# Two key chunks per visit in an attention that runs beside a mixer, and key bucket numbers by three products

## Chip, core and metric

The kernel runs on one NeuronCore of a Trainium2 chip. The metric is the device time of the program in microseconds. A core has TensorE (matrix products, PE in the profile), VectorE (DVE), ScalarE (ACT), GpSimd (POOL) and SyncE (SP, which issues most DMAs). Products are written to PSUM, which has eight banks; everything else lies in SBUF.

## What is computed

A hashed attention, followed by a Fourier mixer with a two-layer perceptron. The attention has 4 batches, 8 heads, 768 rows of 64 channels. Each query and key row gets a bucket number from 6 sign bits, and a query weighs only the keys of its own bucket:

```python
q_bits = (np.einsum('bhsd,dk->bhsk', q, proj) > 0).astype(np.int64)
k_bits = (np.einsum('bhsd,dk->bhsk', k, proj) > 0).astype(np.int64)
q_bucket = np.sum(q_bits * powers, axis=-1)
k_bucket = np.sum(k_bits * powers, axis=-1)
mask = q_bucket[:, :, :, None] == k_bucket[:, :, None, :]
scores = np.where(mask, scale * np.matmul(q, k.transpose(0, 1, 3, 2)), -1000000000.0)
attn = softmax(scores)            # written out in the reference
out = np.matmul(attn, v)
```

The result, as 4 x 768 rows of 512 channels, goes through

```python
mixed = np.real(np.fft.fft(np.fft.fft(x, axis=1), axis=2))
u = x + mixed
un = (u - mu) / np.sqrt(var + 1e-06)
return u + np.maximum(un @ w_ch1, 0.0) @ w_ch2
```

## The kernel before

Heads go in pairs: pair n = 0 to 15, four pairs a batch, `n // 4` the batch. The two heads of a pair lie on partitions 0 to 63 and 64 to 127. Keys are cut into six chunks c of 128, queries into two halves g of 384.

One visit of the attention, for one pair and one chunk, does this. `weigh` (L871) issues four score products (L893), 64 rows deep, so that the two heads run side by side in the array, each query half into one PSUM tile of two banks from the pool `ps_sc` (two such tiles). ScalarE takes the exponential of each half (L897) into a weights buffer `pk`; there are two of these, used in turn. For pairs 5 to 15 VectorE then masks the weights, one instruction per head (L903): it compares the bucket numbers of the queries, `qb`, with that of the key on each partition, `kb`, and multiplies. VectorE adds the masked weights to `acc` (L988), from which the row sums come. `values` (L909) later issues four products of the weights with v (L914), 64 columns wide, so that here too the two heads run side by side, into two PSUM banks from `ps_o` that gather all six chunks. After the last chunk `scale` (L919) adds up `acc` by products with ones (L932) and divides.

Every f32 product shows in the profile as two passes, so a visit's scores are 8 instructions, and its values too.

In `attention` (L955) the values of a chunk are issued in the visit after its own: a visit is scores of c, then values of c-1. The list `pending` holds what is still to do. After each visit the generator yields, and the main loop (L1500 on) issues a few steps of the mixer of the batch before, about 2.3 a visit: these are called fill below. Fill goes through stages: folds, `cs` products (L1086, emptied by ScalarE), A and B products (L1115, both emptied by VectorE, L1129), first-layer products (L1390, emptied by ScalarE, with sums on VectorE), second-layer products (L1270, emptied half by VectorE, L1282, half by ScalarE). All their PSUM tiles come from `pt`, during the attention from a pool `ps_1` of two banks. The generator `ahead` = `prepare(n+1)` (L755) is advanced in chunks 1 to 5; it makes the next pair's transposed q and k, the sign bits (L825, one bank of `ps_1`), `qb` (L839, two tiles of `ps_sc`) and `kb` (L849, one tile of `ps_sc`, copied to SBUF by VectorE at L853).

The order on each engine in batches 1 to 3 is made by a planner, ahead of time: at each moment it issues the instruction, among those that it reckons ready, that stands first in the program. Two things change that. `issue_after` puts an instruction behind a given one on its engine, and `high_priority` moves it ahead of what stands up to 500 places before it. `behind()` does both with the matmul kept in `last[0]`; in batches 1 to 3 it glues the scores of a visit together (all but the first) and the values to them. In batch 0 the order is the program's own. Batches 0 and 1 have other surroundings: loads and conversions of the weights run beside them.

Of the kernel before, what the change touches and what calls it, by code (L numbers as in the profile page):

```python
# [11 lines left out]
F32 = mybir.dt.float32  # L12
# [8 lines left out]
P = 128  # L21
# [464 lines left out]
def _main(  # L486
# [112 lines left out]
    for h in range(2):  # L599
        nc.sync.dma_start(pj[h * D : (h + 1) * D, h * NBITS : (h + 1) * NBITS], proj)  # L600
    pw = const.tile([P, 2, P], BF16, tag="pw", name="pw")
    ones = const.tile([P, 32], F32, tag="ones", name="ones")
    nc.gpsimd.memset(ones, 1.0)
    mhalf = const.tile([P, 1], F32, tag="mhalf", name="mhalf")
# [150 lines left out]
    def prepare(n):  # L755

        lite = n in LITE
        ts = {}
        for io, nm in enumerate("qk"):
            tn = nat.pop((nm, n))  # L760
            tt = wt([P, S], F32, nm + "t", f"{nm}t{n}")
            if n > 0:
                to, at = tt, tn
                if nm == "q":

                    to = tt.rearrange("p (i r n) -> p r i n", i=2, r=2)
                    at = tn.rearrange("p (r i n) -> p r i n", i=2, r=2)
                nc.vector.transpose(to, at)
            for g in range(2) if n == 0 else ():
                ps = pt([P, 3, P], f"tr{nm}{n}_{g}")  # L770
                for i in range(3):
                    c = 2 * i + g if nm == "q" else 3 * g + i
                    nc.tensor.transpose(ps[:, i, :], tn[:, c * P : (c + 1) * P], ident)
                if nm == "q":
                    for i in range(2):
                        dst = tt[:, i * HALF + g * HALF // 2 : i * HALF + (g + 1) * HALF // 2]
                        evac(
                            dst.rearrange("p (j c) -> p c j", c=3),
                            ps[:, :, i * D : (i + 1) * D],
                        )  # L780
                else:
                    evac(
                        tt[:, g * HALF : (g + 1) * HALF],
                        ps.rearrange("p c t -> p (c t)"),
                    )
            ts[nm] = tt
            yield
            norm(n, io, tn)
        if lite:

            qk = wt([P, 2, S], BF16, "qb", f"qkb{n}")
            qz = qk[:, 0].rearrange("p (g s) -> p g s", g=2)
            bits = {"q": qz[:, 0], "k": qk[:, 1, 0:HALF]}
            for io, nm in enumerate("qk"):
                ps = pt([P, HALF], f"bits{nm}{n}")
                for j in range(4):
                    h, g = divmod(j, 2)  # L800
                    nc.tensor.matmul(
                        ps[32 * j : 32 * j + 32, :], pjw[:, h * D : h * D + 32],
                        ts[nm][:, g * HALF : (g + 1) * HALF], start=True, stop=True,
                    )
                nc.vector.tensor_scalar(
                    bits[nm], ps, 0.0, off[:, io : io + 1],
                    op0=ALU.is_gt, op1=ALU.subtract,
                )
                if io == 0:
                    for g in (1, 0):  # L810
                        nc.vector.tensor_scalar(
                            qz[:, g], qz[:, 0], own[:, g : g + 1], None, op0=ALU.mult
                        )
                else:
                    for j in range(4):
                        to, at = (slice(32 * i, 32 * i + 32) for i in (j, j ^ 1))
                        nc.vector.tensor_copy(qk[to, 1, HALF:S], qk[at, 1, 0:HALF])
                yield
            preps[n] = ts["q"], ts["k"], qk, None
            return  # L820

        ps = pt([P, HALF], f"bits{n}")
        for j in range(4):
            src = ts["qk"[j // 2]][:, (j % 2) * HALF : (j % 2 + 1) * HALF]
            nc.tensor.matmul(  # L825
                ps[32 * j : 32 * j + 32, :], pj, src, start=True, stop=True
            )
        bt = wt([P, HALF], BF16, "bt", f"bt{n}")
        nc.vector.tensor_scalar(bt, ps, 0.0, None, op0=ALU.is_gt)  # L829
        yield  # L830

        qb = wt([P, 2, S], BF16, "qb", f"qb{n}")
        kb = wt([P, 2, NT], F32, "kb", f"kb{n}")
        for h in range(2):
            ps = ps_sc.tile([P, 2, 512], F32, tag="sc", name=f"qb{n}_{h}")
            for g in range(2):
                rows = slice(32 * g, 32 * g + 32)
                with behind() if g + h else nullcontext():
                    last[0] = nc.tensor.matmul(  # L839
                        ps[:, g, 0:HALF], pw[rows, h, :], bt[rows, :],  # L840
                        start=True, stop=True,
                    )
            evac(qb[:, h, :].rearrange("p (g s) -> p g s", g=2), ps[:, :, 0:HALF])
        ps = ps_sc.tile([P, 2, 512], F32, tag="sc", name=f"kb{n}")
        for c in range(NT):
            g, i = divmod(c, NT // 2)
            rows = slice(64 + 32 * g, 96 + 32 * g)
            with behind() if c else nullcontext():
                last[0] = nc.tensor.matmul(  # L849
                    ps[:, g, 2 * i : 2 * i + 2], bt[rows, i * P : (i + 1) * P],  # L850
                    pw[rows, :, 0], start=True, stop=True,
                )
        nc.vector.tensor_copy(  # L853
            kb.rearrange("p h (g i) -> p g i h", g=2),
            ps[:, :, 0:NT].rearrange("p g (i h) -> p g i h", h=2),
        )
        preps[n] = ts["q"], ts["k"], qb, kb

# [6 lines left out]
    @contextmanager  # L865
    def behind():

        with tc.issue_after(last[0].ins), tc.high_priority(offset=AHEAD):
            yield

    def weigh(n, c):  # L871

        qt, kt, qb, kb = preps[n]
        ks = slice(c * P, (c + 1) * P)
        heads = [slice(h * D, (h + 1) * D) for h in range(2)]
        pk = pks[npk[0] % NPK]
        npk[0] += 1
        for g in range(2):
            qs = slice(g * HALF, (g + 1) * HALF)
            ps = ps_sc.tile([P, 2, 512], F32, tag="sc", name=f"sc{n}_{g}_{c}")  # L880
            if kb is None:

                at = (c + (NT // 2 if g else 0)) % NT * P
                for h, rows in enumerate(heads):
                    nc.tensor.matmul(
                        ps[:, h, 0:HALF], qb[rows, 1, at : at + P],
                        qb[rows, 0, g * HALF : (g + 1) * HALF],
                        start=True, stop=False,
                    )

            for h, rows in enumerate(heads):
                with behind() if g + h and n >= NPAIR else nullcontext():
                    last[0] = nc.tensor.matmul(  # L893
                        ps[:, h, 0:HALF], kt[rows, ks], qt[rows, qs],
                        start=kb is not None, stop=True,
                    )
            nc.scalar.activation(  # L897
                pk[:, g, :, 0:HALF], ps[:, :, 0:HALF], AF.Exp, scale=SCALE
            )
        if kb is not None:  # L900
            for h in range(2):
                w = pk[:, :, h, 0:HALF]
# [6 lines left out]
    def values(n, c, pk, oos):  # L909

        for g in range(2):
            w = HALF + 1 - g
            for h in range(2):
                nc.tensor.matmul(  # L914
                    oos[g][h * D : (h + 1) * D, 0:w], nat["v", n][:, (2 * c + h) * D : (2 * c + h + 1) * D],
                    pk[:, g, h, 0:w], start=(c == 0), stop=(c == NT - 1),
                )

    def scale(n, oos, sums):  # L919

# [34 lines left out]
    def attention(b):  # L955
# [11 lines left out]
        for t in range(NPAIR):  # L967
# [5 lines left out]
            oos = [ps_o.tile([P, 512], F32, tag="o", name=f"oo{n}_{g}") for g in range(2)]  # L973
            acc = wt([P, 2, 2, HALF], F32, "acc", f"acc{n}", 1)
            first = None
            for c in range(NT):
                pk = weigh(n, c)
                new = pk[:, :, :, 0:HALF]
                sums = [acc]
                if c == 0:  # L980
# [4 lines left out]
                else:  # L985

                    for g in (0, 1) if b == 0 else (slice(0, 2),):
                        nc.vector.tensor_tensor(  # L988
                            acc[:, g], (first if c == 1 else acc)[:, g], new[:, g],
                            op=ALU.add,  # L990
                        )

                for sc in scales:
                    next(sc, None)
                scales.clear()
                while pending:
                    finish()
                for sc in scales if b else ():
                    next(sc, None)
                pending.append((n, c, pk, oos, sums))  # L1000
                if c > (3 if b == 1 else 2):
                    next(half, None)
                if c > 0:
# [477 lines left out]
    with tc.manual_schedule(engines={ET.PE, ET.DVE, ET.Activation, ET.Pool}):  # L1481
# [8 lines left out]
        pwf = wt([P, 2, P], F32, "ef", "pwf", 1)  # L1490
        nc.sync.dma_start(pwf, cn["pw"].ap())
        nc.scalar.copy(pw, pwf)
        means = []
        late = [(f, average(f)) for f in range(DFF // 2, DFF, WC)]
        for _, avg in late:
# [98 lines left out]
```

## Time and profile before

| | us |
|---|---|
| median of 3 runs | 1098.81 |
| lowest and highest | 1097.87, 1100.31 |
| the profiled execution | 1099.06 |
| its span in the trace | 1097.1 |
| TensorE busy | 1044.5 |
| VectorE busy | 790.7 |
| ScalarE busy | 499.3 |
| score products L893, busy | 155.3 |
| value products L914, busy (two forms) | 91.0 + 85.4 |
| exponentials L897, one | 0.81 |
| mask L903, one of a visit's two | 1.01 |
| sum L988, over both halves | 1.75 |

The span is what the profiler saw from the first to the last instruction; the time has about 2 us around it. In a line of the timeline the columns are start, length, engine, line, operation, what is written and read, rows x columns of the array, shape, and how many instructions were merged; brackets hold the idle time before and what ended it. The ends of matmuls are modelled, so what an operation costs TensorE is read from start to start.

### The profile page before, as it was taken

The page shows a single profiled execution, that of the slowest core. Times are in us where ns is not written, and L with a number is a line of the kernel's source. Part 1 is how long each engine was busy: PE and PEld are TensorE (multiplying, and loading weights), DVE is VectorE, ACT ScalarE, POOL GpSimd, SP SyncE. Part 2 cuts the span into 40 slices and gives each one's busy share as a digit, 9 for nine tenths or more (in the row PEclk, how much of TensorE's full clock was granted, in tenths as well). Part 3 has the DMA queues.
Part 4 walks back from the last instruction along what each step waited for, and adds up shares of the span by engine and source line. Part 5 has one row for each costly group of instructions (what it writes and reads, how often), then busy time and mean ns, then how long its engine had stood idle before and what let it go on. Part 6 is the DMA issues. An engine that isn't in the chain of part 4 may idle for free.

```text
span 1097.1 us, 14139 instructions
## 1 busy us (share of the span) xinstructions
PE 1044.5 (95%) x4933; PEld 633.2 (58%) x4933; DVE 790.7 (72%) x1336; ACT 499.3 (46%) x1055; POOL 58.4 (5%) x132
## 2 busy tenths in 40 slices
PE   7989897999989999999999999999999999999997
PEld 3333354446744675545664576645674569768676
DVE  5899958878599977776767785965856775744353
ACT  6987555653276324454326433355315532341430
POOL 0000000002000020010000011001000002100000
PEclk9999999999999999999999999999999999999999
DMA  9755353450056161322144134213032205122401
GB/s 225 222 96 126 63 133 79 141 168 13 20 155 209 45 203 24 68 63 66 26 157 108 48 74 161 44 39 95 16 119 75 68 28 173 50 86 71 140 20 41
DMA packets 175710, 103.13 MB, mean 94 GB/s; under 512 B 129552, under 2 KB 162960, under 8 KB 175632
## 3 DMA queue, kind: packets, MB, share of 16 engines
q1 hardware_dynamic: 169840, 88.65, 30.2%
q0 software_dynamic: 4224, 13.11, 3.7%
q8 instruction: 41, 0.67, 0.3%
q10 hardware_dynamic: 1568, 0.39, 0.2%
q14 instruction: 37, 0.30, 0.1%
HBM read 81.14 MB, written 20.97 MB: 93 GB/s over the span
## 4 chain that ended last, share of the span: by engine, by line
PE 61%; DVE 12%; ACT 4%; issue 2%; DMA 2%; DVEq 0%; SPq 0%; ACTq 0%
PE o L1270 23%; PE h_p L1390 19%; PE oo L914 6%; PE sc L893 6%; DVE pk L903 3%; PE cs L1086 2%; PE A L1115 2%; DMA zraw<-in_moe_w_ch_dram 2%; PE B L1115 1%; DVE acc L988 1%; ACT rr L948 1%; DVE w L1282 1%; DVE h L1256 1%; PE bits L825 1%; PE un L1141 1%
## 5 line engine op out<-in xcount | busy, mean ns | idle before, releaser
L1270 PE MATMUL o<-w,h 128*128 128x256 f32 x1152 | 259.4, 382 | 1.2 <-ACT tq L1289 0.7
L1270 PEld LDWEIGHTS o<-w,h 128*128 128x128 f32 x1152 | 216.3, 190 | 43.6 <-issue 4.6
L897 ACT ACTIVATE pk<-sc 128x768 f32<-128x768 f32 x192 | 147.4, 808 | 77.8 <-PE sc L893 60.2
L1390 PE MATMUL h_p<-x,w 128*128 128x384 f32 x448 | 163.3, 494 | 2.9 <-ACT h L1412 1.5
L914 PE MATMUL oo<-pk,vn 128*64 128x385 f32 (+1 forms) x768 | 155.8, 500 | 5.9 <-DVE pk L903 3.3
L893 PE MATMUL sc<-qt,kt 64*128 64x384 f32 x768 | 155.3, 507 | 5.6 <-ACT pk L897 5.3
L903 DVE SCALAR_TENSOR_TENSOR pk<-qb,kb,pk 128x768 f32<-128x768 bf16 x132 | 129.0, 1013 | 29.9 <-ACT pk L897 29.7
L1390 PEld LDWEIGHTS h_p<-x,w 128*128 128x128 f32 x448 | 82.3, 190 | 70.4 <-ACT pk L897 5.4
L988 DVE TENSOR_TENSOR acc<-acc,pk 128x1536 f32<-128x1536 f32 (+1 forms) x72 | 105.7, 1482 | 7.2 <-ACT pk L897 6.7
L1390 PE MATMUL h_p<-w 128*128 128x384 f32 x288 | 105.5, 489 | 2.3 <-ACT w L1427 2.3
L914 PEld LDWEIGHTS oo<-pk,vn 128*64 128x64 f32 x768 | 49.1, 136 | 100.0 <-issue 69.8
L893 PEld LDWEIGHTS sc<-qt,kt 64*128 64x128 f32 x768 | 66.9, 188 | 50.3 <-issue 23.1
L1390 PEld LDWEIGHTS h_p<-w 128*128 128x128 f32 x288 | 53.7, 190 | 41.7 <-ACT w L1427 3.5
L1282 DVE SCALAR_TENSOR_TENSOR w<-o,rs,w 128x256 f32<-128x256 f32 x56 | 26.7, 479 | 41.6 <-PE o L1270 41.6
L1300 ACT COPY tq<-o 128x256 f32<-128x256 f32 x24 | 8.9, 372 | 105.0 <-PE o L1270 105.0
L1270 PE MATMUL o<-w 128*128 128x256 f32 x176 | 42.3, 383 | 1.3 <-DVE w L1282 1.3
L1416 DVE TENSOR_TENSOR h<-h 128x384 f32<-128x384 f32 x32 | 17.8, 556 | 32.7 <-ACT h L1415 32.7
L1289 ACT COPY tq<-o 128x256 f32<-128x256 f32 x24 | 8.9, 371 | 69.3 <-PE o L1270 69.3
L1270 PEld LDWEIGHTS o<-w 128*128 128x128 f32 x176 | 32.8, 190 | 8.8 <-DVE w L1282 2.9
L1423 DVE TENSOR_TENSOR h<-h 128x384 f32<-128x384 f32 x32 | 17.7, 553 | 27.0 <-ACT h L1422 27.0
L1024 POOL DMA_DIRECT2D out_dram<-w x30 | 16.3, 547 | 388.7 <-issue 293.2
L1086 PE MATMUL cs<-ch,z 128*128 128x128 f32 (+3 forms) x192 | 33.6, 327 | 3.0 <-DVE bt L829 1.9
(170 smaller groups left out, 1314.1 us busy)
## 6 DMA issues: line engine op xcount, KB each, us to landing
w<-ad SPq DMA_DIRECT2D x168, 128.0 KB, 2.0
w<-bd SPq DMA_DIRECT2D x42, 512.0 KB, 4.6
zraw<-in_moe_w_ch_dram POOLq DMA_DIRECT2D x16, 512.0 KB, 3.9
bd<-w SPq DMA_DIRECT2D x14, 512.0 KB, 4.0
vn<-in_v_dram SPq DMA_DIRECT2D x32, 192.0 KB, 3.3
qn<-in_q_dram SPq DMA_DIRECT2D x120, 48.0 KB, 2.4
kn<-in_k_dram SPq DMA_DIRECT2D x60, 96.0 KB, 3.3
zraw<-in_moe_w_ch_dram SPq DMA_DIRECT2D x8, 512.0 KB, 5.9
```

The lines of the kernel that those rows point to most:

```text
L893: last[0] = nc.tensor.matmul(ps[:, h, 0:HALF], kt[rows, ks], qt[rows, qs], start=kb is not None, stop=True,)
L897: nc.scalar.activation(pk[:, g, :, 0:HALF], ps[:, :, 0:HALF], AF.Exp, scale=SCALE)
L903: nc.vector.scalar_tensor_tensor(w, qb[:, h].rearrange("p (g s) -> p g s", g=2), kb[:, h, c : c + 1], w, op0=ALU.is_equal, op1=ALU.mult,)
L914: nc.tensor.matmul(oos[g][h * D : (h + 1) * D, 0:w], nat["v", n][:, (2 * c + h) * D : (2 * c + h + 1) * D], pk[:, g, h, 0:w], start=(c == ...
L988: nc.vector.tensor_tensor(acc[:, g], (first if c == 1 else acc)[:, g], new[:, g], op=ALU.add,)
L1086: nc.tensor.matmul(ps[:, pc + 2 * lo : pc + 2 * hi - 1 : 2], z[:, cp, pc, par, t * P : (t + 1) * P], ch[:, cp, pc, lo:hi], start=(cp == 0) ...
L1115: nc.tensor.matmul(ps[:, cols], F[:, par, k, t, j * P : (j + 1) * P], sq[:, t, k, cols], start=(t == 0), stop=(t == 1),)
L1270: nc.tensor.matmul(ps, a[:, r], right7[i][:, r], start=start and r == 0, stop=r == HF // 2 - 1, skip_group_check=not start,)
L1282: nc.vector.scalar_tensor_tensor(t[:, cols], src, r, t[:, cols], op0=ALU.mult, op1=ALU.add)
L1390: nc.tensor.matmul(ps, left[:, k], right[i][:, k], start=start and k == 0, stop=k == 1, skip_group_check=not start,)
L1416: nc.vector.tensor_tensor(c21, c12, c21, op=ALU.add)
L1423: nc.vector.tensor_tensor(c22, c21, c22, op=ALU.add)
```

## The change

In batches 2 and 3 (pairs from `TWO = 8`) a visit takes two chunks: scores of c, values of c-2 and of c-1, scores of c+1, in this order and glued; then two rounds of fill, since the loop still yields once a chunk. The exponentials of c come between the two values in the program, so that the values of c-2 have read the weights buffer that they write. Batches 0 and 1 keep one chunk a visit.

The key bucket numbers: instead of six products of 32 rows, in a score tile, three products of all 128 rows with a weight matrix `pwk` of two columns for each half, zero outside the rows of that half, in a tile of `ps_1`. The query bits' rows meet zeros.

```diff
+    pwk = const.tile([P, 2, 2], BF16, tag="pwk", name="pwk")
+    nc.gpsimd.memset(pwk, 0.0)
...
-        ps = ps_sc.tile([P, 2, 512], F32, tag="sc", name=f"kb{n}")
-        for c in range(NT):
-            g, i = divmod(c, NT // 2)
-            rows = slice(64 + 32 * g, 96 + 32 * g)
-            with behind() if c else nullcontext():
-                last[0] = nc.tensor.matmul(
-                    ps[:, g, 2 * i : 2 * i + 2], bt[rows, i * P : (i + 1) * P],
-                    pw[rows, :, 0], start=True, stop=True,
-                )
+        ps = pt([P, NT // 2, 2, 2], f"kb{n}")
+        for i in range(NT // 2):
+            nc.tensor.matmul(
+                ps[:, i], bt[:, i * P : (i + 1) * P], pwk, start=True, stop=True
+            )
...
-    def weigh(n, c):
+    TWO = 8
+
+    def scores(n, c, glued=False):
...
-                with behind() if g + h and n >= NPAIR else nullcontext():
+                with behind() if (g + h or glued) and n >= NPAIR else nullcontext():
...
-            nc.scalar.activation(
-                pk[:, g, :, 0:HALF], ps[:, :, 0:HALF], AF.Exp, scale=SCALE
-            )
+            if n < TWO:
+                weights(pks[npk[0] % NPK], g, ps)
+            pss.append(ps)
+        return pss
+
+    def weights(pk, g, ps):
+
+        nc.scalar.activation(
+            pk[:, g, :, 0:HALF], ps[:, :, 0:HALF], AF.Exp, scale=SCALE
+        )
+
+    def weigh(n, c, pss):
+
+        qb, kb = preps[n][2:]
+        pk = pks[npk[0] % NPK]
+        npk[0] += 1
+        for g in range(2) if n >= TWO else ():
+            weights(pk, g, pss[g])
...
-                nc.tensor.matmul(
+                oo = nc.tensor.matmul(
...
+        last[0] = oo
...
-            for c in range(NT):
-                pk = weigh(n, c)
+            def chunk(c, pss):
+
+                nonlocal first
+                pk = weigh(n, c, pss)
...
+                elif c % 2 == 0:
+                    pss = scores(n, c)
+                    if len(pending) > 1:
+                        finish()
+                    new = [chunk(c, pss)]
+                    if pending:
+                        finish()
+                    new.append(chunk(c + 1, scores(n, c + 1, True)))
+                    for sc in scales:
+                        next(sc, None)
+                    scales.clear()
+                    pending += new
...
+        for g in range(2):
+            rows = slice(64 + 32 * g, 96 + 32 * g)
+            nc.scalar.copy(pwk[rows, g], pwf[rows, :, 0])
```

`chunk` is the old body of the loop up to the sum into `acc`; `finish` takes the oldest entry of `pending` and issues its values, and after a pair's last chunk its `scale`.

More of the change, by code (lines that the diff above doesn't have):

```diff
@@ L843, in prepare @@
             evac(qb[:, h, :].rearrange("p (g s) -> p g s", g=2), ps[:, :, 0:HALF])
-        ps = ps_sc.tile([P, 2, 512], F32, tag="sc", name=f"kb{n}")
-        for c in range(NT):
-            g, i = divmod(c, NT // 2)
-            rows = slice(64 + 32 * g, 96 + 32 * g)
-            with behind() if c else nullcontext():
-                last[0] = nc.tensor.matmul(
-                    ps[:, g, 2 * i : 2 * i + 2], bt[rows, i * P : (i + 1) * P],
-                    pw[rows, :, 0], start=True, stop=True,
-                )
+        ps = pt([P, NT // 2, 2, 2], f"kb{n}")
[3 more added lines that the diff above has]
+            )
         nc.vector.tensor_copy(
             kb.rearrange("p h (g i) -> p g i h", g=2),
-            ps[:, :, 0:NT].rearrange("p g (i h) -> p g i h", h=2),
+            ps.rearrange("p i g h -> p g i h"),
         )
@@ L869, in behind @@
             yield
-    def weigh(n, c):
+    TWO = 8
+    def scores(n, c, glued=False):
         qt, kt, qb, kb = preps[n]
+        pss = []
         ks = slice(c * P, (c + 1) * P)
         heads = [slice(h * D, (h + 1) * D) for h in range(2)]
-        pk = pks[npk[0] % NPK]
-        npk[0] += 1
         for g in range(2):
@@ L991, in attention @@
                         )
[L993 to L1000, printed above, removed]
+                return n, c, pk, oos, sums
+            for c in range(NT):
+                if n < TWO:
+                    new = chunk(c, scores(n, c))
+                    for sc in scales:
+                        next(sc, None)
+                    scales.clear()
+                    while pending:
+                        finish()
+                    for sc in scales if b else ():
+                        next(sc, None)
+                    pending.append(new)
+                elif c % 2 == 0:
[4 more added lines that the diff above has]
+                    if pending:
+                        finish()
+                    new.append(chunk(c + 1, scores(n, c + 1, True)))
+                    for sc in scales:
+                        next(sc, None)
+                    scales.clear()
+                    pending += new
                 if c > (3 if b == 1 else 2):
```

## The prediction

> **What bounds the kernel now.** I read the page first (busy shares and the 40 slices), then the chain of waits, then the timeline of TensorE around several visits of the attention, then a table of stretches for VectorE. The page:
>
> ```profile
> PE 1044.5 (95%) x4933; PEld 633.2 (58%) x4933; DVE 790.7 (72%) x1336; ACT 499.3 (46%) x1055; POOL 58.4 (5%) x132
> ...
> PE   7989897999989999999999999999999999999997
> ...
> PE 61%; DVE 12%; ACT 4%; issue 2%; DMA 2%; DVEq 0%; SPq 0%; ACTq 0%
> ```
>
> The attention of batches 2 and 3 runs from 407 to about 923 us beside the mix of the batch before; there every slice of TensorE is a 9, and the end is set by TensorE. But its matmul ends are modelled, so "busy" hides the price of a change of array shape. That price is read from the starts of groups:
>
> ```profile
> 521.64 3.72 PE L1270 MATMUL o<-w,h 128*128 128x256 f32 x16
> 525.29 1.56 PE L893 MATMUL sc<-qt,kt 64*128 64x384 f32 x8
> 526.78 1.51 PE L914 MATMUL oo<-pk,vn 128*64 128x385 f32 x8
> 528.22 3.72 PE L1270 MATMUL o<-w,h 128*128 128x256 f32 x16
> ```
>
> A pass over 384 columns takes 0.32 us in a long run (the chain of waits has L1390 x112 in 36.12 us), one over 256 columns 0.213. The 8 score passes run in pairs side by side (64 rows each), so they stream 4 x 0.32 = 1.28 us; the next group starts 1.49 after them: 0.21 is lost. The 8 value passes also stream 1.28, and the next starts 1.44 later: 0.16 lost. The 16 passes of fill stream 3.41 and scores follow at 3.65: 0.24 lost. So each visit pays fill to scores 0.24, scores to values 0.21, values to fill 0.16: 0.61 us. I worked out the same differences from all starts between 415 and 945 us; they repeat within some hundredths almost everywhere, and waits over 0.4 us there add up to under 10 us. The two transitions that the change brings in are in the trace too:
>
> ```profile
> 407.31 1.56 PE L893 MATMUL sc<-qt,kt 64*128 64x384 f32 x8
> 408.80 1.16 PE L1086 MATMUL cs<-ch,z 128*128 128x129 f32 x8
> ...
> 97.11 1.51 PE L914 MATMUL oo<-pk,vn 128*64 128x385 f32 x8
> 98.55 0.34 PE L885 MATMUL sc<-qkb 64*128 64x384 bf16 x2
> ```
>
> Scores to fill costs 1.49 - 1.28 = 0.21, values to scores 1.44 - 1.28 = 0.16 (to the bf16 scores of batch 0, same shape of array as the f32 ones).
>
> **What the Trainium skill says.** "TensorEngine Tiling (Array Packing)", Key Properties: changing the tiling mode drains the TensorE, changing the tile within it does not. The trace agrees: 0.16 to 0.24 us at each change of shape, none between passes of one shape. The same page, Gotcha 1: row tiles write to different PSUM banks, which raises the pressure on PSUM; here the two score tiles take four of the eight banks. "TensorE: Matmul & The Clock Gate", Architectural detail: ScalarE and VectorE are strict FIFOs, so whatever is queued behind a mask waits for it.
>
> **The change part by part.** Sums are made against the profiled execution, 1099.06 us (span 1097.1 and 1.96 around it); the median of the runs is 1098.81, so the two agree within 0.3.
>
> (1) Fewer changes of shape. Per two chunks before: 2 x 0.61 = 1.22. After: fill to scores 0.24, scores to values 0.21, values to values 0, values to scores 0.16, scores to fill 0.21 = 0.82. A batch before: 0.45 for its first chunk (no values yet), 23 x 0.61, and 0.40 for the values left at its end: 14.9. After: 0.45, 11 x 0.82, 0.40: 9.9. Saved 5.0 a batch, 10.0 for two. The passes themselves, exponentials, masks and sums stay the same in number; no DMA is moved past another, though each load of the next pair stands beside visits at other times.
>
> Does the second group of scores find its buffers free? Both score buffers are filled by the first chunk. Put its start at 0: scores end at about 0.9 and 1.5; the exponential of query half 0 also needs the weights buffer that the values of chunk c-2 read, free at 1.49 + 0.69 + about 0.17 = 2.35. It takes 0.81 (the page's 808 ns), so the two end near 3.2 and 4.0. The 16 value passes end at 1.49 + 2.56 = 4.05; the new scores start at 4.21 and 4.85. Slack about 0.85: one ScalarE copy of 0.48 in between fits, two do not. Then fill is put between, and a break costs 0.16 + 0.24 - 0.16 = 0.24. Before, 4 of 46 visits are broken (scores x4, A/B products x2, scores x4 at 437.28 is one). I take 4 breaks of 24: give back 1.0.
>
> (2) A stage where VectorE sets the pace gains nothing:
>
> ```profile
> 430.00:440.00 10.00, 9.11 (x58) 6.64 (x58) 9.48 (x15) 1.94 (x3) 0.00 (x0) 1.00 0.00 0
> 440.00:450.00 10.00, 10.00 (x60) 6.75 (x58) 10.00 (x14) 3.12 (x6) 0.00 (x0) 1.00 0.40 75
> ```
>
> (columns: us, then busy us of PE, PEld, DVE.) In the A/B stage VectorE is at 9.5 to 10 of 10; there are four chunks, so two double visits, a batch: 4 x 0.41 = give back 1.6.
>
> (3) Key bucket numbers. Before, six products of 32 rows between fill; starts 566.42 and 566.58 with fill at 564.93 ahead give fill to them 0.21 and them to fill 0.16 in all: 0.37 per pair. After, three bf16 products over the full array, no change of shape; the trace has no such product of 2 columns. Bounds: a bf16 weight load of half the rows takes 0.09 (L885), so three exposed ones 0.28, none exposed about 0.05. I take 0.27; saved 0.10 x 11 pairs = 1.1 (bounds 1.0 and 3.5). They leave the score buffers too, and with that this wait goes, seen in both batches:
>
> ```profile
> 432.92 0.50 PE L839 MATMUL qb<-bt,pw 32*128 32x384 bf16 x4
> 434.31 0.24 PE L849 MATMUL kb<-pw,bt 32*128 32x2 bf16 x6 [0.89 <-ACT qb L537]
> ```
>
> 2 x 0.89 = 1.8. What is late next there is the copy of the key numbers on VectorE, behind masks, holding one of the two banks that fill uses; that is in (4). The set-up (one GpSimd fill, two ScalarE copies of 32 x 2, nearest row 0.197) lies at about 119 us beside weight loads, where nobody waited for the copy of pw: 0, at most 0.4.
>
> (4) The new wait. Masks 2 x 1.01 and a sum of 1.75 make 3.8 us of VectorE per chunk; two chunks in a row make 7.6. Fill has two PSUM banks, and the second-product steps (L1270) empty half of their banks on VectorE. Before:
>
> ```profile
> 510.77 1.90 DVE L903 SCALAR_TENSOR_TENSOR pk<-qb,kb,pk 128x768 f32<-128x768 bf16 x2
> 512.59 0.68 DVE L1256 TENSOR_TENSOR h<-h 128x512 f32<-128x512 f32 x1
> 513.20 1.75 DVE L988 TENSOR_TENSOR acc<-acc,pk 128x1536 f32<-128x1536 f32 x1
> ...
> 516.00 1.99 PE L1270 MATMUL o<-w 128*128 128x256 f32 x8 [0.55 <-DVE w L1282]
> ```
>
> Already a burst of 3.8 costs 0.55 to 0.72 in one visit of each batch. After, fill restarts 5.9 us into a visit and masks and sums keep VectorE until about 11.4; a product takes 1.71. Depending on which step comes first, TensorE runs out of banks for 0.9 or 2.6 us, 1.75 on average. About 7 of the 24 double visits stand there: 12.3. In the A/B stage both banks go to one step and VectorE empties both: fill of 2.8 ends at 8.7, the banks come free at 12.5: 3.8 x 4 = 15.2. All together 27.5 if nothing else fills the hole. But the planner issues whatever is ready, and the next visit's scores and values are: their buffers are free from 6.5, chunk c is masked at 5.9. So I take a tenth, 2.7; bounds 0 and 27.5. Behind a waiting mask stand the evacuations on VectorE, and behind those TensorE: that is the price just counted.
>
> Sum: -10.0 + 1.0 + 1.6 - 1.1 - 1.8 + 2.7 = -7.6: **1091.5 us**.
>
> **Rivals.** *Bursts win (slower).* The mechanism of (4), in the second-product and A/B stages, decides once it costs over 10.3 / 24 = 0.43 us per double visit. For it: VectorE is at 72% overall and full in the A/B stage. Against: hardly any wait of TensorE on VectorE now. At 0.6 of the full price: 1099.06 - 10.3 + 16.5 = 1105; at all of it 1116. *The gluing fails.* ScalarE is late in most visits, fill comes between: 0.24 + 0.21 + 0.16 + 0.24 + 0.21 = 1.06 instead of 1.22, 0.16 x 22 = 3.5 saved; with 2.9 of (3) and 2.7 of (4): 1095.4. Against: ScalarE is at 46%. *Even.* (4) costs about 10: 1098.5.
>
> **How the numbers follow.** Forecast 0.48, gluing fails 0.16, even 0.06, bursts 0.30. A measurement of this kernel can tell 0.2% (2.2 us) from no change. Faster: 0.48 + 0.14 = 0.62; same 0.02 + 0.06 = 0.08; slower 0.30. The likeliest case's own range is 1085 (10.0, 1.8 and 2.3 of (3), nothing given back) to 1095. To leave out no more than 2 in 10 it must reach into the bursts: 1085 to 1106.
>
> **What would show it.** Right: L893 and L914 starts in the order scores, values x16, scores, with 1.49, 2.72 and 1.49 us to the next; kb in full-array shape without a gap. Wrong: "[... <-DVE w L1282]" or "<-DVE x L1129" before TensorE fill in the double visits, scores x4 broken by fill, or scores waiting for L897 over 0.2 us.

## The result and the profile after

| | before | after |
|---|---|---|
| median of 6 runs, us | 1098.26 | 1112.91 |
| lowest and highest | 1097.15, 1100.31 | 1107.93, 1113.22 |
| span of the profiled execution | 1097.1 | 1111.0 |

The ratio is 1.0108, with an interval of 1.0088 to 1.0128: the change makes the kernel slower by 1.1%. The forecast was 1091.5, and the result lies above its range.

The page of the kernel after: busy time, and the chain of waits by engine.

```profile
PE 1042.4 (94%) x4900; PEld 635.6 (57%) x4900; DVE 789.2 (71%) x1336; ACT 499.1 (45%) x1057; POOL 56.7 (5%) x133
...
PE 48%; DVE 16%; ACT 3%; issue 2%; DMA 0%; DVEq 0%; ACTq 0%
```

The work is the same: 33 products fewer (three instead of six for 11 pairs), and every engine is busy within 2.4 us of what it was. So the time isn't spent on more work; it is spent on waits. The chain says whose: but its shares of the span can't be set beside those of the page before, since the chain could be followed back to 212 us before and only to 330 after. From 330 us on, which both cover, the pieces of the chain add up to 618 us of TensorE before and 538 after, and to 91 us of VectorE before and 174 after.

To place it I cut each trace at the first score product of every batch, and at the first `cs` product of the last mix:

| us | start | batch 0 | batch 1 | batch 2 | batch 3 | last mix |
|---|---|---|---|---|---|---|
| before | 12.1 | 106.1 | 289.1 | 259.4 | 256.9 | 173.5 |
| after | 11.0 | 107.6 | 293.0 | 265.1 | 261.4 | 172.9 |

Batch 2 is 5.7 longer, batch 3 4.5. Another 4.3 is lost before batch 2 begins, where only the key numbers are new.

The array shapes went as the change meant them to. The timeline of TensorE after, around one double visit, and around the key products of pair 9:

```profile
420.33 1.56 PE L892 MATMUL sc<-qt,kt 64*128 64x384 f32 x8
421.82 2.81 PE L928 MATMUL oo<-pk,vn 128*64 128x385 f32 x16
424.56 1.56 PE L892 MATMUL sc<-qt,kt 64*128 64x384 f32 x8
...
443.98 0.92 PE L892 MATMUL sc<-qt,kt 64*128 64x384 f32 x4
444.83 0.23 PE L848 MATMUL kb<-pwk,bt 128*128 128x4 bf16 x3
445.66 1.22 PE L1149 MATMUL A<-sq,F 128*128 128x193 f32 x6 [0.60 <-DVE x L1163]
```

Scores to values 1.49, values x16 to scores 2.74, scores to what follows (at 426.05) 1.49: the forecast had 1.49, 2.72, 1.49. In the last three lines the scores are broken off, the key products take 0.23, and TensorE then stands for want of a bank. The waits of TensorE from 400 to 925 us, by what ended them, show how far that goes (columns: engine, what it was to write and its line, what it waited for, us in total, times, longest). After:

```profile
PE A L1149 <- DVE x L1163: 4.3, 4, 1.6
PE h_p L1424 <- ACT w L1473: 3.2, 4, 1.0
PE h_p L1424 <- ACT w L1461: 2.3, 2, 1.1
PE un L1175 <- DVE x L1163: 1.7, 4, 0.6
PE cs L1120 <- ACT F L1133: 1.4, 1, 1.4
PE oo L928 <- DVE pk L917: 1.4, 2, 0.7
PE h_p L1424 <- ACT h L1446: 1.2, 2, 0.6
PE o L1304 <- DVE tq L1350: 1.0, 2, 0.5
```

The same view of the kernel before has four lines: 2.3 us for the first layer (L1427), 1.8 for the key products, 1.3 for the second products, 0.9 for the first layer again; none for A, `un` or the values. Nearly every stage of fill now waits on the emptying of a bank, by VectorE or by ScalarE. Which part of the change brings which of these lines is what the experiments ask.

### The profile page after: what moved, and what is told of

Its sections match the earlier page's. It is cut to its first block, busy times and chain, and to the rows that moved or that the text cites. A ratio compares the mean times of both kernels' runs of the same rounds, so it can differ in the third digit from the quotient of the medians.

```text
span 1111.0 us, 14089 instructions
## 1 busy us (share of the span) xinstructions
PE 1042.4 (94%) x4900; PEld 635.6 (57%) x4900; DVE 789.2 (71%) x1336; ACT 499.1 (45%) x1057; POOL 56.7 (5%) x133
## 4 chain that ended last, share of the span: by engine, by line
PE 48%; DVE 16%; ACT 3%; issue 2%; DMA 0%; DVEq 0%; ACTq 0%
PE o L1304 21%; PE h_p L1424 14%; DVE pk L917 5%; PE oo L928 4%; DVE acc L1005 4%; PE sc L892 4%; PE cs L1120 2%; ACT pk L903 1%; PE A L1149 1%; PE B L1149 1%; DVE x L1163 1%; ACT rr L963 1%; DVE h L1462 1%; PE bits L827 1%; PE sum L947 1%
## 5 line engine op out<-in xcount | busy, mean ns | idle before, releaser
L928 PE MATMUL oo<-pk,vn 128*64 128x385 f32 (+1 forms) x768 | 152.1, 496 | 7.2 <-DVE pk L917 5.4
L928 PEld LDWEIGHTS oo<-pk,vn 128*64 128x64 f32 x768 | 51.5, 136 | 97.3 <-issue 76.9
L1334 ACT COPY tq<-o 128x256 f32<-128x256 f32 x24 | 8.9, 372 | 115.1 <-PE o L1304 115.1
L1350 DVE TENSOR_TENSOR tq<-tq,o 128x256 f32<-128x256 f32 x24 | 10.1, 419 | 35.3 <-PE o L1304 35.2
```

The source lines that it names most:

```text
L928: oo = nc.tensor.matmul(oos[g][h * D : (h + 1) * D, 0:w], nat["v", n][:, (2 * c + h) * D : (2 * c + h + 1) * D], pk[:, g, h, 0:w], start=( ...
```

## The experiments

Each ratio is to the kernel before on the same chip. Kernels e1 to e4 ran beside 29 runs of it with a median of 1101.04, f1, f3, f4 and f5 beside 29 with 1101.33, g1 to g4 beside 36 with 1101.03. Lengths of batches, holds and waits come from the one traced run of each kernel; in batches 2 and 3 its granted clock is 1.00 everywhere but in e3. There such lengths repeat well: f1, g2 and g4, which are the same in these batches, take 257.6 and 254.7 us in all three traces.

### Each half alone

e1, the key numbers alone: the kernel before, with only this.

```diff
-        ps = ps_sc.tile([P, 2, 512], F32, tag="sc", name=f"kb{n}")
...
+        ps = pt([P, NT // 2, 2, 2], f"kb{n}")
+        for i in range(NT // 2):
+            nc.tensor.matmul(
+                ps[:, i], bt[:, i * P : (i + 1) * P], pwk, start=True, stop=True
+            )
```

> One chunk a visit as before, only the key bucket numbers by three full-array products in a bank of fill. Bursts theory (the loss comes from 7.6 us of masks and sums in a row on VectorE): within 3 us of before in batches 2 and 3, and whatever the change loses in batch 1 (3.4 us between 130 and 411 us of its trace) shows here too, since nothing else of the change reaches batch 1: 1098 to 1103. Keys theory (the bank that the key numbers take from fill is the loss): most of the 14 us is here, 1105 to 1112.

Measured: 1103.96, ratio 1.0029 (1.0018 to 1.0040). Alone, the cheaper key products already lose 3 us. Batches 2 and 3 are 1.2 and 1.1 longer. Against the 1101.0 that the kernel before took here, this fits the bursts theory and not the keys theory. The timeline of TensorE in e1 shows two things that the forecast had not:

```profile
437.52 0.92 PE L891 MATMUL sc<-qt,kt 64*128 64x384 f32 x4 [0.89 <-ACT qb L537]
...
447.90 0.92 PE L1113 MATMUL B<-sq,F 128*128 128x193 f32 x4 [0.31 <-DVE kb L851]
```

The 0.89 us wait for the copy of `qb`, that the key products had, is now the scores': they need the same score tile. And B waits directly for the copy of the key numbers, which holds the bank.

e2, the visits alone: the change, with the six key products back in their score tile.

```diff
-        ps = pt([P, NT // 2, 2, 2], f"kb{n}")
...
+        ps = ps_sc.tile([P, 2, 512], F32, tag="sc", name=f"kb{n}")
+        for c in range(NT):
```

> Two chunks a visit in batches 2 and 3, the key bucket numbers as before. Bursts theory: batches 2 and 3 lose about 8 to 12 us as in the changed kernel, batches 0 and 1 nothing: 1106 to 1110. Keys theory: faster than before, 1090 to 1096, since the saved changes of shape stay.

Measured: 1097.08, ratio 0.9967 (0.9949 to 0.9984). The visits alone are faster by 4 us, and neither half alone explains a loss of 11 to 15. The waits of TensorE from 400 to 925 us in e2:

```profile
PE A L1151 <- DVE x L1165: 4.2, 4, 1.6
PE h_p L1426 <- ACT w L1463: 2.3, 2, 1.1
PE oo L930 <- DVE pk L919: 1.4, 2, 0.7
PE h_p L1426 <- ACT w L1475: 1.1, 2, 0.6
PE o L1306 <- DVE w L1318: 1.1, 3, 0.6
```

The waits of A and of the values are there in full, so these are the price of the bursts. The waits for F, for `un` on x, for the copy h at L1446 and two thirds of that for w at L1473 are not: they come with the key tile, or with the other order that the planner makes around it. (For `un` the key tile isn't needed: f3 below, which has none in a fill bank, waits 1.7 there too.)

e3, the change once more, unedited, on the same chip.

> The changed kernel once more, beside the others on one chip. Its times fell in two groups, 1108 and 1113. Both theories: the same again; the trace of the other group would show whether the 5 us lie in batches 0 and 1, where weight loads run beside the attention, or in batches 2 and 3.

Measured: 1115.45, ratio 1.0103 (1.0063 to 1.0144). So the loss holds in a second set of runs, and it isn't the sum of the halves: 0.9967 times 1.0029 would be 0.9996.

e4, the change, with the second chunk's masks and sum put behind the first round of fill, to cut the burst of 7.6 us in two.

```diff
-                    new.append(chunk(c + 1, scores(n, c + 1, True)))
+                    pk1 = weigh(n, c + 1, scores(n, c + 1, True), True)
...
+                else:
+                    mask(n, c, pk1)
+                    pending.append(add(c, pk1))
```

> The whole change, but the masks and the sum of a visit's second chunk stand in the program after the first round of fill instead of before it; TensorE's products and ScalarE's exponentials are as in the change. Bursts theory: the new waits of TensorE in batches 2 and 3 (8 us a batch) fall by more than half while the saved changes of shape stay: 1094 to 1103. Keys theory: no better than the change, 1108 to 1114. Chance-of-order theory (any rearrangement by the planner moves the time by some us): anything, with waits in other places.

Measured: 1106.75, ratio 1.0047 (1.0025 to 1.0069): about half of the loss goes, and the time lies above what the bursts theory expected and below what the keys theory did. That alone would speak for bursts as a cause; f3 below has to be read with it.

### The tile of the key numbers

f1, the whole change, three products and all, but in a score tile and glued.

```diff
-        ps = pt([P, NT // 2, 2, 2], f"kb{n}")
+        ps = ps_sc.tile([P, 2, 512], F32, tag="sc", name=f"kb{n}")
+        ps = ps[:, 0, 0 : 2 * NT].rearrange("p (i g h) -> p i g h", g=2, h=2)
         for i in range(NT // 2):
-            nc.tensor.matmul(
-                ps[:, i], bt[:, i * P : (i + 1) * P], pwk, start=True, stop=True
-            )
+            with behind() if i else nullcontext():
+                last[0] = nc.tensor.matmul(
```

> The whole change, but the three key products write a score tile, glued, as the six of before did, and not a bank of fill. If the loss is the bank taken from fill (bank theory): close to the visits alone, 0.995 to 1.000 of before. If it is the products themselves or their set-up: as the change, 1.008 to 1.013.

Measured: 1096.70, ratio 0.9954 (0.9937 to 0.9971). One tile taken from the other pool turns the loss of 1.1% into a gain of half a per cent. The products are not at fault, their place is. One thing goes along with the place: in f1 the key products are glued and moved ahead, as before the change, which had dropped both. No run has glued products in a fill bank. Two runs below speak against the gluing as the cause: g1 leaves the six key products glued and only adds a turn in a fill bank, which costs, and g3 leaves them unglued in the fill bank and gets most of the loss back.

f3, the visits alone (e2) with the edit of e4.

> Two chunks a visit, key numbers as before, the second chunk's masks and sum after the first round of fill. What is left of the bursts theory: visits alone still wait 7.3 and 6.1 us in batches 2 and 3 against 5.1 and 4.2 before; if half of the 7.6 us row on VectorE is what they wait for, the waits fall to those of before and the time to 0.992 to 0.995 of before. If the waits are placed by the planner and only move: 0.996 to 1.000.

Measured: 1099.86, ratio 0.9996 (0.9986 to 1.0007). Without the key tile in a fill bank, cutting the bursts gains nothing and loses about 3 us against e2. With the key tile there, in e4, the same edit helped. Set e4 against f3, as the change against e2: with the bursts cut, the key tile in a fill bank costs 2.6 us in batch 2 and 1.5 in batch 3, where with whole bursts it costs 7.1 and 6.3. The copy of the key numbers also came sooner in e4: the bank of pair 11 was held 2.3 us instead of 4.2, that of pair 9 0.4 instead of 1.6. Which of the two, the shorter burst or the shorter hold, did it isn't separated.

f4, the visits alone, but not for pairs 8 and 12, which stand in the A/B stage.

```diff
-    TWO = 8
+    TWO = (9, 10, 11, 13, 14, 15)
...
-                if n < TWO:
+                if n not in TWO:
```

> Two chunks a visit with the key numbers as before, but not in the first pair of a batch (pairs 8 and 12), whose visits stand beside the products that VectorE empties in pairs (A and B). Bursts theory: the waits for x there (1.9 us a batch in the visits alone) go, at the price of three saved changes of shape (1.2 us a batch): 0.994 to 0.997. If the A and B stage is not special: 0.997 to 0.999.

Measured: 1098.00, ratio 0.9965 (0.9943 to 0.9987). The same as e2 by whole runs; by the traces, e2 is 0.5 us shorter in batch 2 and 0.6 in batch 3. Part (2) had two of the three double visits of such a pair gain nothing and the third 0.4. The waits show what eats the gain: f4 has no wait of A on x, where e2 has 4.2 us, and has the 1.8 of the key products for `qb` again.

f5, the whole change, with the copy of the key numbers on ScalarE.

```diff
-        nc.vector.tensor_copy(
+        nc.scalar.copy(
```

> The whole change, but ScalarE copies the key numbers out of the bank of fill instead of VectorE. If the bank is held because the copy waits behind masks and sums on VectorE: half of the loss or more goes, 1.000 to 1.005 of before. If taking a turn among the two banks is enough, however short it is held: 1.006 to 1.012.

Measured: 1103.71, ratio 1.0023 (1.0012 to 1.0035). Most of the loss goes. In batches 2 and 3 the bank is held 0.4 to 1.0 us, once 2.7. What remains is earlier: batch 2 is 259.9 and batch 3 256.9, as before the change, while batches 0 and 1 are 7.0 longer together in its trace.

### The bank's holder, and a version to keep

g1, the visits alone, with a spare turn added: three products over the whole array into a fill bank, emptied by a copy on VectorE that nothing reads.

```diff
+        spare = wt([P, 2, NT], F32, "spare", f"spare{n}")
+        ps = pt([P, NT // 2, 2, 2], f"turn{n}")
+        for i in range(NT // 2):
+            nc.tensor.matmul(
+                ps[:, i], bt[:, i * P : (i + 1) * P], pw[:, :, 0:2], start=True, stop=True
+            )
+        nc.vector.tensor_copy(
```

> Two chunks a visit, the key numbers as before in a score tile, and beside them three spare full-array products into a bank of fill with a copy by VectorE that nothing reads: the turn of the change without its use. Bank theory: 7 us more in each of batches 2 and 3 than the visits alone less what the moved key products saved, so 1.005 to 1.012 of before. If the turn costs only its own instructions (3 products, about 0.3 us a pair): 0.998 to 1.001.

Measured: 1108.53, ratio 1.0058 (1.0039 to 1.0076), 0.9% above e2, for products of 0.23 us and a copy of 0.17 a pair. Batch 2, with the bank held 1.9, 1.5, 6.0 and 3.5 us, is 5.9 longer than in e2; batch 3, with 1.9, 1.5 and 1.5, only 1.4, where 7 had been expected in each. Short holds cost little there; the loss goes with the long ones.

g2 is f1 with the two small set-up copies on GpSimd instead of ScalarE.

```diff
-            nc.scalar.copy(pwk[rows, g], pwf[rows, :, 0])
+            nc.gpsimd.tensor_copy(pwk[rows, g], pwf[rows, :, 0])
```

> Two chunks a visit, three key products in a score tile, and the weights for them set up by GpSimd instead of ScalarE, where they stood in front of the copy that the mean products wait for (0.5 us later in the change). Expected: 0.993 to 0.996 of before, about 0.5 us under the same with ScalarE. If the set-up is not on the path: no different from it.

Measured: 1096.64, ratio 0.9960 (0.9946 to 0.9973), as f1.

g3, the whole change, with nothing else than the copy put first.

```diff
-        nc.vector.tensor_copy(
-            kb.rearrange("p h (g i) -> p g i h", g=2),
-            ps.rearrange("p i g h -> p g i h"),
-        )
+        with tc.high_priority(offset=AHEAD):
+            nc.vector.tensor_copy(
+                kb.rearrange("p h (g i) -> p g i h", g=2),
+                ps.rearrange("p i g h -> p g i h"),
+            )
```

> The whole change, but the copy of the key numbers is put ahead of what stands up to 500 places before it on VectorE. If the bank is held by masks and sums in front of the copy: as with the copy on ScalarE or better, 0.999 to 1.004 of before. If VectorE's row is not what holds it: 1.007 to 1.013, as the change.

Measured: 1099.40, ratio 0.9981 (0.9970 to 0.9993). The same products in the same bank, the same copy on the same engine, and in the program only the place of the copy is another: 1.0103 becomes 0.9981. The planner answers with another order on TensorE too, of which more below. The timelines of VectorE and TensorE around pair 11 show what was moved. After:

```profile
574.01 1.76 DVE L1005 TENSOR_TENSOR acc<-acc,pk 128x1536 f32<-128x1536 f32 x1
...
574.40 0.23 PE L848 MATMUL kb<-pwk,bt 128*128 128x4 bf16 x3
575.69 0.95 DVE L535 CAST qb<-qb 128x768 bf16<-128x768 f32 x1
576.56 1.94 DVE L917 SCALAR_TENSOR_TENSOR pk<-qb,kb,pk 128x768 f32<-128x768 bf16 x2
...
578.41 0.17 DVE L851 COPY kb<-kb 128x12 f32<-128x12 f32 x1
```

The products are done at 574.63. The copy takes 0.17 but stands behind a sum, the copy of `qb` and two masks, and ends at 578.58: one of fill's two banks is held 4.2 us for twelve columns. In g3:

```profile
568.82 0.23 PE L848 MATMUL kb<-pwk,bt 128*128 128x4 bf16 x3
568.91 0.95 DVE L535 CAST qb<-qb 128x768 bf16<-128x768 f32 x1
...
569.05 1.56 PE L1425 MATMUL h_p<-x,w 128*128 128x384 f32 x4
569.78 0.17 DVE L852 COPY kb<-kb 128x12 f32<-128x12 f32 x1
```

Held 1.1 us, and fill follows the key products after 0.23. The waits of TensorE from 400 to 925 us in g3:

```profile
PE A L1150 <- DVE x L1164: 3.1, 2, 1.6
PE h_p L1425 <- ACT w L1462: 2.3, 2, 1.1
PE un L1176 <- DVE x L1164: 1.7, 4, 0.6
...
PE h_p L1425 <- ACT w L1474: 1.1, 2, 0.6
```

The wait for w is back at the 1.1 of e2, and those for F and for the copy h before the first layer, 1.4 and 1.2 in the kernel after, have no line; `un` still waits 1.7, as in f3.

g4 is g2 with double visits from pair 5, so in batch 1 too.

```diff
-    TWO = 8
+    TWO = 5
```

> As the version with the three products in a score tile and the set-up on GpSimd, but two chunks a visit from pair 5 on, so in batch 1 too. Changes of shape theory: three pairs more, 9 double visits less 0.4 us each, 3 us under it: 0.990 to 0.993 of before. Against: in batch 1 the weights arrive and are converted beside the attention, TensorE waits there 25 us anyway, and the saving may be absorbed: 0.994 to 0.998.

Measured: 1104.35, ratio 1.0036 (1.0019 to 1.0053), worse than both expectations. Batch 1 takes 293.5 instead of 290.5 in g2, and its TensorE waits rise to 31.9 us from 25.1 before the change (my sum, as in the next section). The waits view of batch 1 has scores waiting 8.9 us for ScalarE's exponentials `pk` (5.3 before the change), and first-layer products 10.3 for its results w and h (3.1 before): two chunks in a row make waits for ScalarE worse. The saving of part (1) needs a stage that doesn't wait.

Five versions beat the kernel before: e2, f1, f4, g2 and, by less, g3. f1 and g2, at 1096.7 and 1096.6 us, have the lowest ratios and are 0.4 us shorter than e2 in each of batches 2 and 3; by whole runs they can't be told from e2 and f4.

## Why the prediction was wrong

I took the starts of TensorE's instructions in batches 2 and 3 apart into waits (the gap beyond the streaming time and the price of a shape change, where a semaphore ended it) and the rest:

| batch 2, batch 3: us | waits | rest | length |
|---|---|---|---|
| before | 5.1, 4.2 | 254.3, 252.7 | 259.4, 256.9 |
| e2, visits alone | 7.3, 6.1 | 250.6, 249.0 | 258.0, 255.1 |
| f1, score tile | 8.0, 6.5 | 249.6, 248.2 | 257.6, 254.7 |
| after | 12.8, 10.9 | 252.3, 250.5 | 265.1, 261.4 |
| g3, copy first | 9.3, 7.5 | 250.3, 249.4 | 259.6, 256.9 |

**Part (1), the shapes, right in kind and 1.6 too large.** With its breaks it forecast -9.0. In e2 the rest, which holds the changes of shape, falls by 3.7 and 3.7, together 7.4; counted change by change at the prices of the starts it is 3.9 and 4.0. That -10.0 + 1.0 + 1.6 is -7.4 as well is chance: the 1.6 of part (2) is time in which TensorE waits, and belongs with the waits. Some of the shortfall can be seen. Before, 5 of the 8 changes to the 32-column products (sign bits and row sums) in batch 2 came straight from the values and cost 0.16 each; in e2 only one does, and 5 come from fill, at 0.31. The Trainium skill, "TensorEngine Tiling (Array Packing)", Key Properties, says that changing the mode drains TensorE. The trace agrees, with these prices.

**Part (2), the stage of VectorE, right**, as f4 shows.

**Part (4), the bursts by themselves, too low, but of the right order.** In e2 the waits rise by 2.2 and 1.9, together 4.1. The two waits of 0.9 for `qb` at the key products are gone there, so the new ones come to 5.9, where the forecast took 4.3: the 1.6 of part (2), and 2.7 of at most 27.5. That is 0.25 us for each of the 24 double visits; the slower rival needed 0.43. They stand in the A/B stage, as said (4.2 in the waits view, none in f4); in the second products, the other place named, the wait is 1.1 in e2 and was 1.3 before.

**Part (3), the saving, right in the sum.** f1 is 0.4 shorter than e2 in each of the two batches, for seven pairs: 0.11 a pair, against 0.10 forecast. So close a match is luck in part: the rest falls by 1.0 and 0.8, which is 0.26 a pair and inside the stated bounds, and new waits of 0.7 and 0.4 take back more than half. The 1.8 for the `qb` waits came too, but not from the key products' new tile: e1, which has it, keeps both waits of 0.89 at its scores, and e2, which hasn't, loses them, by the other order of its visits.

**The step that failed** is the end of (3): "What is late next there is the copy of the key numbers on VectorE, behind masks, holding one of the two banks that fill uses; that is in (4)". It named the mechanism, and gave it no price: (4) was worked out for masks and sums alone, with both of fill's banks in use by fill. Against e2 the key tile in its fill bank costs 7.1 us in batch 2 and 6.3 in batch 3, 13.4 together, where (3) had -1.1 for the products, -0.7 of it in these two batches. That is 14.1 of the 17.4 us by which batches 2 and 3 miss the forecast (+10.2 against -7.2); the 1.6 of the shapes and the 1.6 of the waits in e2 make up the remainder within 0.1. (In the trace of e3, the same kernel, batch 3 takes 261.4 again. Batch 2 takes 268.0, but that says nothing about the bank: the 2.9 more all lie between 421 and 428 us, 1.3 in the wait for F at the start of the batch, and 1.6 where the trace has the granted clock at 0.50 for 3.4 us.) As a comparison of whole runs: 1.0103 with the bank held, 0.9981 with the copy first, 0.9954 with no fill bank taken at all.

Nor is it the hold alone. e1 holds the bank as long (1.2 to 4.8 us in batches 2 and 3; after, 1.5 to 4.2), and is only 1.2 and 1.1 longer than before. With double visits the price is six times that, and with the bursts cut (e4 against f3) it is 4.1. The reading that fits is that a long hold then meets the long stretch of masks and sums in which VectorE empties the other bank late as well. Bursts and bank were priced one at a time, and their meeting wasn't.

Where the 13.4 stand is less simple than "TensorE waits for the key bank". Directly behind key products there is 0.60 at 445.66 and 0.6 at 635 (the wait of the second product for w) in batch 2. The others stand where the two banks turn over at other moments than in e2. The timeline after, in the first-layer stage, more than 25 us from any key product, shows such a one:

```profile
605.08 1.02 DVE L917 SCALAR_TENSOR_TENSOR pk<-qb,kb,pk 128x768 f32<-128x768 bf16 x1
...
606.48 1.01 DVE L917 SCALAR_TENSOR_TENSOR pk<-qb,kb,pk 128x768 f32<-128x768 bf16 x1
...
607.41 0.55 DVE L1462 TENSOR_TENSOR h<-h,w 128x384 f32<-128x384 f32 x1
...
607.99 0.52 ACT L1463 ACTIVATE h<-h 128x384 f32<-128x384 f32 x1 [2.05 <-DVE h L1462]
608.42 0.46 ACT L1473 COPY w<-h_p 128x384 f32<-128x384 f32 x1
...
608.94 1.56 PE L1424 MATMUL h_p<-w 128*128 128x384 f32 x4 [1.02 <-ACT w L1473]
```

VectorE's sum of h stands behind the masks. ScalarE's next instruction needs it and stands 2.05 us, and the copy queued behind that one is what empties TensorE's bank. This is the strict queue of ScalarE and VectorE that the Trainium skill describes ("TensorE: Matmul & The Clock Gate", Architectural detail), quoted in the forecast for the masks only. Here it runs over two engines: a bank that ScalarE empties waits for VectorE too. The forecast had counted only the banks that VectorE empties itself.

The split into waits and rest leaves a gap here: in the kernel after, the rest is 1.7 and 1.5 above that of e2 with as many changes of shape. Waits too short for the split would show so; that isn't shown.

**The order, a rival that stays.** The planner makes the order ahead of time from what it reckons free, so a bank held in its plan moves fill elsewhere, and a shorter hold (f5, g3) changes plan and hardware together. The traces show how much. Leave out the key products and go through the other 2311 products of batches 2 and 3 in order: f1 has the same as e2 at every place, g3 another one at 148 places, the kernel after at 836. The number of moved products doesn't set the loss by itself: e1 differs from the kernel before at 484 places and loses 2.3 us, g1 from e2 at 336 and loses 7.3. How much of the 13.4 is the bank itself and how much the other order isn't separated; a kernel with the order of e2 written out by hand and the key tile in a fill bank would do it, and wasn't tried.

**The set-up, small.** Forecast 0, at most 0.4. The two copies of 0.39 together stand ahead of the copy that the mean products wait for. The timeline after:

```profile
120.01 0.39 ACT L1529 CAST pwk<-pwf 32x2 bf16<-32x2 f32 x2
...
121.06 1.98 PE L674 MATMUL wm<-part,mean 128*128 128x512 f32 x4 [1.63 <-ACT part L671]
```

Before, that wait was 1.10: 0.5 more. g2 avoids it and is no faster than f1 by what these runs can tell.

**Batches 0 and 1, open.** After comes to batch 2 4.3 us late. Up to 1.7 of it is the granted clock: in batches 0 and 1 the trace has a clock of 0.50 for 10.2 us before and for 13.7 us after, and the 3.4 us more take at most 1.7 us from TensorE. 0.5 is the set-up. Batch 0 takes 107.0 to 110.6 in eight of the nine traces with the new key products, 106.0 to 106.7 in four of the five without; but g4, which has them, takes 106.5, and g1, which hasn't, 109.9. Loads of weights run beside these stages, and no run here sorts these apart.

**The rivals.** *Bursts win* named the right side and its interval of 1105 to 1116 holds the result, but not for its reason: with all its bursts, e2 is faster than before. *The gluing fails* isn't what happened: shape changes fall from 100 to 78 in batch 2 as in e2 (79).

## What to carry to other kernels

When a small result moves into a ring of two PSUM banks, price the time that it holds one: from its product to the end of its copy in the queue of the engine that empties it, not the copy's own 0.17 us. Put that copy ahead of the long work on its engine, or give the tile a place that the bound engine isn't waiting for. When two changes load the same resource, one by long bursts and one by a held bank, work out the case in which they meet, and count the banks that another engine empties only after the busy one has delivered. Where a planner makes the order from what it reckons free, compare the orders before and after too: a held bank also moves other work.

## What the hardware showed beyond that

- Three bf16 products of 4 columns over the whole array, each with its own weights, take TensorE 0.23 us from the first start to the next fill product (568.82 to 569.05 in g3), when nothing is waited for.
- In these traces the granted clock is not a little lower everywhere: it is 1.00, except for stretches of 3.4 or 6.8 us at 0.50 and the last 5 to 9 us. All but one of the stretches lie in batches 0 and 1. The one in batch 2, in e3, cost 1.6 us with TensorE busy throughout.
- The spread between runs of one kernel goes with the granted clock. In the 29, 29 and 36 runs of the kernel before, a mean clock lower by 0.001 goes with a time longer by 0.73, 0.64 and 0.53 us (correlation -0.81, -0.77, -0.66). Of the six runs of the kernel after, the two at 1108 us had 0.994, the four at 1113 had 0.991 to 0.992; that slope, 1.9 us for each 0.001, is more than the clock alone gives in the other kernel. e3 shows 1.6 us for a stretch that lowers the mean by 0.0015, about 1 for each 0.001; the rest is not explained.
